# A Fourier layer with a routed feed-forward part: the first stage folded onto 64x64 tiles, its scratch tensor stored as twice 64 rows, and zero rows written from 120 partitions

## Chip, cores and metric

The kernel runs on one core of a Trainium2 chip. The metric is the time of one execution on the device in microseconds, given as the median of several runs. One execution was also profiled.

## The reference

```python
def _attn_ref(x, w_r, w_i, b_r, b_i):           # x: 8 x 3136 x 256
    X = np.fft.rfft(x, axis=1)
    Yr = Xr @ w_r - Xi @ w_i + b_r               # Xr, Xi: real and imaginary part
    Yi = Xr @ w_i + Xi @ w_r + b_i
    lam = 0.01                                   # soft threshold of both
    Yr = np.sign(Yr) * np.maximum(np.abs(Yr) - lam, 0.0)
    Yi = np.sign(Yi) * np.maximum(np.abs(Yi) - lam, 0.0)
    return np.fft.irfft(Yr + 1j * Yi, n=3136, axis=1)

def _moe_ref(x, w_gate, w1, w2, capacity):       # capacity 128, per batch
    scores = np.einsum('bsd,d->bs', x, w_gate)
    out = x.copy()
    top_idx = np.argpartition(-scores[b], capacity)[:capacity]
    h = np.maximum(x[b, top_idx] @ w1, 0.0)
    out[b, top_idx] = x[b, top_idx] + sigmoid(scores[b, top_idx])[:, None] * (h @ w2)
```

## The kernel before

A sequence of 3136 samples is taken as 98 rows of 32 (`N1`, `N2`), and the transform is done in two stages each way. For each of the 8 batches:

- **First stage**, `ld_x` and `s1`: an x tile holds 98 rows on partitions and 8 of the 32 columns, each of 256 channels. One batch has four tiles and eight units (`U`); a unit multiplies four columns by the 98x98 table `w` (line 400, two matmuls of 512 columns in float32) into the PSUM tile `s` and copies it out (line 405). After every second unit the result goes to the scratch tensor `As` in DRAM (lines 411 and 412: 96 rows and 2 rows).
- **Second stage** and the work in the frequency domain, per group g of 13 (`G`): `ld_a` loads `av` from `As` with the columns on partitions, one load for two groups; `s2` makes the spectrum (line 446, PSUM tile `px`), split into a high part `Xh` (ScalarE, 452) and a low part `Xl` (VectorE, 453); `spectral` multiplies by the weights (lines 228 to 230): a common product into `pcb`, copied by ScalarE to `ks` (467), from which GpSimd makes `kb` (469, with the bias), and two products into `py`, to which VectorE adds `kb` (473). `shrink` gives `Y` (ScalarE 478, VectorE 480). `s2i` transforms back into `pca` and `pcb` (498), ScalarE copies them to `ct` (505), VectorE forms the scores (`junk`, 507), and `ct` goes to the scratch tensor `Cs`.
- **Last stage**, `ld_c` and `s1i`: 128-row tiles `cv` of `Cs` (twice 64 rows, of which 49 count) are multiplied by `wi_sb` as four matmuls of 49 rows on quarters of the array (line 556), copied (558) and stored to the output.
- **Routing**: `select` and `place` find the 128 highest scores on VectorE with small matmuls, then GpSimd gathers the rows, two matrix products follow, and the rows are scattered back.

The order of each engine's work is the order of the code. The main loop runs over steps t, one group each: step t issues the stores left by step t - 1 (`flush`), loads, then `s2(t + 1)`, a unit of `s1` or `s1i` (`pair`), `spectral(t)`, the late DMAs on ScalarE's queue, `s2i(t - 1)`, `shrink(t)` and a second unit. Batches 2 to 7 of the first stage run `LEAD` = 17 steps ahead of their groups, about eight units in 13 steps, at t = 9 to 87; the units of batch 1 stand in steps 1 to 8, those of batch 0 ahead of the loop. The x loads stand four steps ahead of the unit, `av` is loaded at t + 3 and has two buffers, x has three.

Nearly all DMAs are issued by SP, in program order; `move` puts every other half of the output on ScalarE's queue instead. DMAs take eight semaphores in turn, so each waits until the eighth before it has landed. At t = 3 `pads` writes zeros into rows 49 to 63 of each half of the three `Cs` tensors, which the last stage loads with the rest: 15 rows of 32 KB six times, all from 15 partitions of one zeroed tile. `warm` runs matmuls and transposes at the very start, while the first x tiles are loaded.

Of the kernel before, what the change touches and what calls it, by code (L numbers as in the profile page):

```python
# [27 lines left out]
def _tables():  # L28
    m = np.arange(NH)
    n2 = np.arange(N2)  # L30
    n4 = np.arange(64)
# [4 lines left out]
    wi = np.zeros((64, 64))
    g = np.zeros((2, 2, N2, NJ - 1, 3, N2))
    gi = np.zeros((2, 2, N2, NP, 2, 2, 64))
    for j in range(NJ - 1):
        e = 2 * j + 2  # L40
        for p, r in enumerate((e, NH - e if e < NH else 0)):
            a = 2 * np.pi * ((n1 * r) % N1) / N1
            wf[:, j, p, 0] = np.cos(a)
            wf[:, j, p, 1] = -np.sin(a)
            for k2 in range(N2):
                k = r + 98 * k2
                sg = 1.0 if 2 * k <= S else -1.0
# [56 lines left out]
def fourier_moe(ctx: ExitStack, tc: tile.TileContext, x, w_r, w_i, b_r, b_i, wg, w1, w2,  # L104
# [21 lines left out]
    w = c_tile([N1, N1], F32, "w")  # L126
# [3 lines left out]
    xts = [c_tile([128, 8, D], F32, "xt" + str(k)) for k in range(3)]  # L130
    cvs = [c_tile([128, 8, D], F32, "cv" + str(k)) for k in range(2)]
# [251 lines left out]
    def ld_x(b, i):  # L383
        if i % 2:
            return
        k = i // 2
        t = xt[b, k] = (xts[:2] + cvs)[k] if b == 0 else xts[(4 * b + k + 1) % 3]
        ld(t[:96], xv[b, :96, 8 * k:8 * k + 8, :])
        ld(t[96:N1], xv[b, 96:, 8 * k:8 * k + 8, :])

    def s1(b, i):
        if i == 0:
            As[b] = dram.tile([N1, N2, D], F32, name="As")
        if i % 2 == 0:
            at[b] = pool.tile([128, 2, 2, 2 * D], F32, name="ot" if b == 0 and i > 3 else "at", bufs=2)
        f = xt[b, i // 2]
# [5 lines left out]
        if b == 0 and i % 2:  # L402
            nc.vector.tensor_copy(t[:N1, i % 2], p[:N1])
        else:
            nc.scalar.copy(out=t[:N1, i % 2], in_=p[:N1])  # L405
# [3 lines left out]
        def store():  # L409
            n = slice(4 * i - 4, 4 * i + 4)  # L410
            nc.sync.dma_start(out=As[b][:96, n, :], in_=t[:96])
            nc.sync.dma_start(out=As[b][96:, n, :], in_=t[96:N1])
        stores.append(store)

    def ld_a(b, g):
        if g == G - 1:
            av[b, g] = pool.tile([64, 1, D], F32, name="av", bufs=2)
            ld(av[b, g][:, 0, :], As[b][96:].rearrange("c n d -> (c n) d"))
        elif g % 2 == 0:
            av[b, g] = av[b, g + 1] = pool.tile([128, 4, D], F32, name="av", bufs=2)  # L420
            ld(av[b, g], As[b][:96].rearrange("(j c) n d -> (c n) j d", c=4)[:, 2 * g:2 * g + 4])

    def s2(b, g):
# [27 lines left out]
        vh, vl = [t.rearrange("p h c (j a s) -> p a (h c) j s", j=2, a=2) for t in (xh, xl)]  # L451
# [82 lines left out]
    def pads():  # L534
        z = pool.tile([128, 2, 2, 2 * D], F32, name="ot", bufs=2).rearrange("p r s (o x) -> p o (r s x)", o=1)
# [32 lines left out]
    def warm():  # L568
# [7 lines left out]
        a = pool.tile([128, 2, 2, 2 * D], F32, name="ot", bufs=2).rearrange("p a b c -> p (a b c)")  # L576
        nc.gpsimd.memset(a, 0.0)
        v = a.rearrange("p (n d) -> p d n", d=64)[:, :16]
        nc.vector.transpose(out=v, in_=v)
        nc.vector.transpose(out=a[:, :512], in_=a[:, :512])  # L580
        nc.vector.transpose(out=v, in_=p[:, 0].rearrange("p (n d) -> p d n", d=16))
        nc.vector.transpose(out=a[:, :512], in_=p[:, 1])

    YB, XB, KB, RB = 2, 2, 1, 1
# [94 lines left out]
    rest = [(b, i) for b in range(B) for i in range(U)]
    for t in range(-1, B * G + 20):  # L680
# [19 lines left out]
        if t == 3:  # L700
            pads()
# [66 lines left out]
```

## Time and profile before

| | |
|---|---|
| median of 3 runs | 826.88 us (819.29 to 827.66) |
| profiled execution | 832.16 us, span of its instructions 830.4 us |
| TensorE, matmuls | 711.4 us busy, 86% |
| VectorE | 478.4 us, 58% |
| ScalarE | 366.7 us, 44% |
| GpSimd | 161.1 us, 19% |
| DMA | 174.46 MB, mean 210 GB/s |
| granted TensorE clock, mean | 0.930 of full |

How to read it: the busy share is a mean over stages. Matmuls overlap, so their times are given as the union of the intervals. A wait counts only where the waiting engine is the one that the rest waits for; a row of the waits names the engine, the line and the releaser inferred from semaphores.

### The profile page before, as it was taken

What the parts mean: (1) busy time and instruction counts of PE and PEld (TensorE: products, weight loads), DVE (VectorE), ACT (ScalarE), POOL (GpSimd) and SP (SyncE); (2) the same over time, 40 slices, a digit from 0 to 9 for tenths busy, and PEclk for the clock granted to TensorE, in tenths of its full rate; (3) what the DMA queues carried; (4) which work ended last, traced back from release to release, by engine and by line L of the source; (5) the groups of instructions that cost most, each with busy time, mean ns of one, the idle gap of its engine ahead of it and who ended that gap; (6) DMA issues with size and microseconds to landing.
All of it is one profiled execution on the core that took longest, in us unless ns stands there. A gap on an engine that the chain in (4) does not pass through costs nothing. (4 is left out here: it accounts for less than half of the span.)

```text
span 830.4 us, 19603 instructions
## 1 busy us (share of the span) xinstructions
PE 711.4 (86%) x7964; PEld 516.1 (62%) x7964; DVE 478.4 (58%) x1333; ACT 366.7 (44%) x663; POOL 161.1 (19%) x148
## 2 busy tenths in 40 slices
PE   8189159999889998999899999999899789878876
PEld 4067137767666666666677677666677677654464
DVE  3335115555446776756646776766548989871640
ACT  2035115555545555545544554655454444432200
POOL 0013012212212221212212212222212122220000
PEclk9679659999999999999999999999999999895679
DMA  9749886679878978878778786888666455557600
GB/s 244 242 141 208 130 260 191 165 249 290 303 229 231 297 217 253 264 217 246 236 235 242 223 240 209 276 247 254 213 194 211 150 167 169 160 151 276 144 18 13
DMA packets 78266, 174.46 MB, mean 210 GB/s; under 512 B 6427, under 2 KB 59640, under 8 KB 67448
## 3 DMA queue, kind: packets, MB, share of 16 engines
q1 hardware_dynamic: 73440, 158.38, 64.1%
q10 hardware_dynamic: 3840, 12.66, 5.5%
q0 software_dynamic: 896, 2.17, 0.9%
q8 instruction: 63, 1.03, 0.5%
q14 instruction: 27, 0.22, 0.1%
HBM read 92.18 MB, written 81.07 MB: 209 GB/s over the span
## 5 line engine op out<-in xcount | busy, mean ns | idle before, releaser
L469 POOL TENSOR_TENSOR kb<-ks,bias 128x512 f32<-128x512 f32 (+1 forms) x104 | 134.1, 1289 | 572.7 <-ACT ks L467 572.7
L473 DVE TENSOR_TENSOR py<-py,kb 128x512 f32<-128x512 f32 (+1 forms) x104 | 72.4, 696 | 129.3 <-POOL kb L469 117.8
L446 PE MATMUL px<-g_sb,av 64*64 64x96 f32 x3072 | 85.9, 248 | 63.3 <-DMA av<-As 41.6
L453 DVE TENSOR_TENSOR Xl<-px,Xh 128x768 fp32r<-128x768 f32 x96 | 91.9, 957 | 72.6 <-ACT Xh L452 72.3
L446 PEld LDWEIGHTS px<-g_sb,av 64*64 64x64 f32 x3072 | 79.0, 136 | 85.4 <-issue 71.1
L505 ACT COPY ct<-pcb 128x256 f32<-128x256 f32 x96 | 35.7, 371 | 199.8 <-PE pcb L498 195.9
L400 PE MATMUL s<-xt,w 98*98 98x512 f32 x232 | 116.4, 625 | 4.3 <-ACT ot L558 4.3
L452 ACT CAST Xh<-px 128x768 fp32r<-128x768 f32 x96 | 77.3, 806 | 64.2 <-PE px L446 64.0
L498 PE MATMUL pca<-Y,gi_sb 64*64 64x256 f32 x768 | 104.4, 391 | 0.0
L498 PE MATMUL pcb<-Y,gi_sb 64*64 64x256 f32 x768 | 104.4, 391 | 0.0
L405 ACT COPY at<-s 98x1024 f32<-98x1024 f32 x58 | 58.9, 1015 | 48.3 <-PE s L400 34.0
L478 ACT ACTIVATE r<-py,m2l 128x512 f32<-128x512 f32 (+1 forms) x104 | 72.5, 697 | 11.5 <-DVE py L473 11.5
L228 PE MATMUL pcb<-wsh,Xh 128*128 128x256 f32 x208 | 76.1, 366 | 0.6 <-DVE Csc L507 0.6
L556 PE MATMUL s<-cv,wi_sb 49*64 49x512 f32 x464 | 68.6, 622 | 6.9 <-ACT ot L558 6.9
L480 DVE SCALAR_TENSOR_TENSOR Y<-py,r 128x512 f32<-128x512 f32 (+1 forms) x104 | 71.2, 685 | 2.1 <-ACT r L478 2.1
L558 ACT COPY ot<-s 128x1024 f32<-128x1024 f32 x58 | 59.2, 1021 | 15.8 <-PE s L556 15.6
L507 DVE CUSTOM_DVE_ANT_0 junk<-pcb,wgb 128x256 f32<-128x256 f32 x96 | 40.5, 422 | 40.9 <-ACT ct L505 40.0
L498 PEld LDWEIGHTS pca<-Y,gi_sb 64*64 64x64 f32 x768 | 45.8, 133 | 26.7 <-issue 2.4
L400 PEld LDWEIGHTS s<-xt,w 98*98 98x98 f32 x232 | 34.2, 166 | 43.6 <-issue 32.2
L228 PE MATMUL py<-wnh,Xh 128*128 128x256 f32 x208 | 59.7, 287 | 0.6 <-DVE Y L480 0.6
L230 PE MATMUL pcb<-wsl,Xh 128*128 128x256 f32 x208 | 59.7, 287 | 0.0
L229 PE MATMUL pcb<-wsh,Xl 128*128 128x256 f32 x208 | 59.7, 287 | 0.0
(135 smaller groups left out, 1369.8 us busy)
## 6 DMA issues: line engine op xcount, KB each, us to landing
cv<-Cs SPq DMA_DIRECT2D x30, 1024.0 KB
av<-As SPq DMA_DIRECT2D x48, 512.0 KB
Cs<-ct SPq DMA_DIRECT2D x96, 256.0 KB
xt<-in_x SPq DMA_DIRECT2D x30, 768.0 KB
As<-at SPq DMA_DIRECT2D x30, 768.0 KB
out<-ot SPq DMA_DIRECT2D x30, 384.0 KB
out<-ot ACTq DMA_DIRECT2D x30, 384.0 KB
Cs<-ot SPq DMA_DIRECT2D x6, 480.0 KB
```

The source lines that it names most:

```text
L228: nc.tensor.matmul(out, wh, mh, start=start, stop=False)
L229: nc.tensor.matmul(out, wl, mh, start=False, stop=False)
L400: nc.tensor.matmul(p[:N1, h, :], w, f[:N1, n:n + 2, :], start=True, stop=True)
L446: nc.tensor.matmul(o[:, :, N2 * j:N2 * j + N2], a[64 * p:64 * p + 64, 2 * (g % 2) + j, 128 * h + 64 * q:128 * h + 64 * q + 64], g_sb[64 * ...
L452: nc.scalar.copy(out=vh, in_=v)
L453: nc.vector.tensor_tensor(out=vl, in0=v, in1=vh.bitcast(F32), op=ALU.subtract)
L469: nc.gpsimd.tensor_tensor(out=kb[:r], in0=ks[:r].broadcast_to([r, 2, D]), in1=bias[:r], op=ALU.add)
L473: nc.vector.tensor_tensor(out=py[:r], in0=py[:r], in1=kb[:r], op=ALU.add)
L478: nc.scalar.activation(out=r1[:r], in_=py[:r], func=AF.Relu, bias=m2l[:r], scale=1.0)
L480: nc.vector.scalar_tensor_tensor(out=y[:r], in0=py[:r], scalar=0.0, in1=r1[:r], op0=ALU.min, op1=ALU.add)
L498: nc.tensor.matmul(p[q][64 * a:64 * a + 64], gi_sb[64 * q:64 * q + 64, g, c, 64 * a:64 * a + 64], y[64 * q:64 * q + 64, c, :], start=(c == ...
L556: nc.tensor.matmul(p[64 * c:64 * c + 64, r, :], wi_sb[64 * r:64 * r + NH], f[64 * r:64 * r + NH, 4 * c + 2 * e:4 * c + 2 * e + 2, :], star ...
```

## The change

- **Fold.** x rows m and m + 49 are added and subtracted (`fold`, two `tensor_tensor` per unit), and the 98-row product becomes two 49-row products, of the sums (c = 0, even rows of the spectrum) and the differences (c = 1, odd ones). A tile has 128 partitions in two halves r of 64, each with four of the tile's columns, so a unit is four matmuls of 49 rows by 64 results on quarters of the array, the form of line 556. Rows 49 to 63 of the tiles are zeroed once. In batch 0 two of three folds run on VectorE, all others on GpSimd, after `spectral` of the step two ahead of the unit.
- **As** has twice 64 rows and is stored with one DMA of 128 partitions; `av` is loaded with two DMAs for two groups (one for each half q), at t + 4 and with three buffers (`AB`).
- **x** is loaded as two halves of 48 rows, the second through `move` on ScalarE's queue, and one DMA for the rows 48; it has two buffers for three.
- **Zero rows** are written from 120 partitions (15 rows of 32 KB, cut into 120 pieces of 4 KB), a pair of DMAs in each of the steps 8, 10 and 12.
- The first stage's copies all run on ScalarE (in batch 0 every second one ran on VectorE); `warm` stands behind the first units and keeps only its matmuls. The tables are reordered to match.

```diff
-    xts = [c_tile([128, 8, D], F32, "xt" + str(k)) for k in range(3)]
-    cvs = [c_tile([128, 8, D], F32, "cv" + str(k)) for k in range(2)]
+    xts, cvs = [[c_tile([128, 8, D], F32, n + str(k)) for k in range(2)] for n in ("xt", "cv")]
+    for k, t in enumerate(xts + cvs):
+        (nc.vector if k % 2 else nc.gpsimd).memset(t[32:64], 0.0)
...
-        ld(t[:96], xv[b, :96, 8 * k:8 * k + 8, :])
-        ld(t[96:N1], xv[b, 96:, 8 * k:8 * k + 8, :])
+        for r in (1, 0):
+            move(r, t[64 * r:64 * r + 48], xv[b, :48, :, 8 * k + 4 * r:8 * k + 4 * r + 4, :])
+        ld(t[48:113:64], xv[b, 48, :, 8 * k:8 * k + 8, :].rearrange("h (r c) d -> r h c d", r=2))
+
+    def fold(b, i, eng):
+        e = i % 2
+        t = xt[b, i // 2][:, :, 2 * e:2 * e + 2, :]
+        f = sd[b, i] = pool.tile([128, 2, 2, D], F32, name="sd", bufs=2)
+        for k, op in enumerate((ALU.add, ALU.subtract)):
+            eng.tensor_tensor(out=f[:113, k], in0=t[:113, 0], in1=t[:113, 1], op=op)
...
-        for h in range(2):
-            n = 4 * (i % 2) + 2 * h
-            nc.tensor.matmul(p[:N1, h, :], w, f[:N1, n:n + 2, :], start=True, stop=True)
+        for r in range(2):
+            for c in range(2):
+                nc.tensor.matmul(p[64 * c:64 * c + 64, r, :], w[64 * r:64 * r + NH, c, :], f[64 * r:64 * r + NH, c], start=True, stop=True)
...
-            nc.sync.dma_start(out=As[b][:96, n, :], in_=t[:96])
-            nc.sync.dma_start(out=As[b][96:, n, :], in_=t[96:N1])
+            nc.sync.dma_start(out=As[b].rearrange("q m n d -> (q m) n d")[:, 4 * i - 4:4 * i + 4, :], in_=t)
...
-            av[b, g] = av[b, g + 1] = pool.tile([128, 4, D], F32, name="av", bufs=2)
-            ld(av[b, g], As[b][:96].rearrange("(j c) n d -> (c n) j d", c=4)[:, 2 * g:2 * g + 4])
+            av[b, g] = av[b, g + 1] = pool.tile([128, 2, 2, D], F32, name="av", bufs=AB)
+            for q in range(2):
+                ld(av[b, g][:, q], As[b][q, :48].rearrange("(j c) n d -> (c n) j d", c=4)[:, g:g + 2])
...
-        for t in Csd:
-            for q in range(2):
-                ld(t[q, NH:].rearrange("m n d -> m (n d)").rearrange("m (k x) -> m k x", k=4), z[:64 - NH].broadcast_to([64 - NH, 4, 2048]))
+        for q in range(2):
+            ld(Csd[k][q, NH:].rearrange("m n d -> (m n d)").rearrange("(p x) -> p x", p=120), z[:120, :1024])
...
-        if 1 < t + 3 < B * G:
-            ld_a(*divmod(t + 3, G))
+        if 1 < t + 4 < B * G:
+            ld_a(*divmod(t + 4, G))
...
-        if t == 3:
-            pads()
+        if t in (8, 10, 12):
+            pads((t - 8) // 2)
...
         issue_late()
+        for b, i in steady(t + LEAD + 2):
+            fold(b, i, nc.gpsimd)
```

What this moves on SP, steps 3 and 4 of the kernel before (`av<-As` is the second-stage load, `Cs<-ot` the zero rows, `at` the first stage's result):

```order
L155 DMA av<-As 128x4x256 [waits DMAHW5_49]
L155 DMA gi_sb<-t_gi 128x512 [waits DMAHW6_49]
L155 DMA Cs_70<-ot 60x1x2048 [waits DMAHW7_49,Pool_49]
L155 DMA Cs_71<-ot 60x1x2048 [waits DMAHW1_49]
L155 DMA Cs_72<-ot 60x1x2048 [waits DMAHW3_49]
L155 DMA g_sb<-t_g 128x384 [waits DMAHW5_49]
L411 DMA As<-at 96x2048 [waits DMAHW6_49,Activation_49]
L412 DMA As<-at 2x2048 [waits DMAHW7_49]
```

There each `Cs<-ot` row stands twice. Of the change, steps 7 and 8:

```order
L153 DMA gi_sb<-t_gi 128x512 [waits DMAHW6_49]
L159 DMA xt_78<-in_x 48x2x1024 [waits DMAHW7_49,Pool_49]
L153 DMA xt_78<-in_x 2x2x1024 [waits DMAHW0_49]
L153 DMA av<-As 32x256 [waits DMAHW2_49,PE_49]
L153 DMA gt_sb<-t_gt 64x192 [waits DMAHW4_49]
L153 DMA Cs_70<-ot 120x1024 [waits DMAHW5_49,Pool_49]
L153 DMA wq<-t_wq 25x392 [waits DMAHW7_49]
```

The zero rows now stand behind all second-stage loads of the first batch, one `Cs` tensor at a time.

GpSimd in the steady steps, before (`kb` of one group after the other, here around the last group of a batch):

```order
L469 TENSOR_TENSOR kb<-ks,bias 128x512 x3
L431 MEMSET Xh 128x6x64
L431 MEMSET Xl 128x6x64
L469 TENSOR_TENSOR kb<-ks,bias 128x512
L469 TENSOR_TENSOR kb<-ks,bias 64x512
```

and with the change, from the same place on (`sd` is the folded tile):

```order
L434 MEMSET Xl 128x6x64
L472 TENSOR_TENSOR kb<-ks,bias 128x512
L395 TENSOR_TENSOR sd<-xt_78 113x512 x2
L472 TENSOR_TENSOR kb<-ks,bias 64x512
L472 TENSOR_TENSOR kb<-ks,bias 128x512
L395 TENSOR_TENSOR sd<-xt_77 113x512 x2
L472 TENSOR_TENSOR kb<-ks,bias 128x512 x2
```

Between two `kb` there are now two adds in eight steps of 13.

ScalarE in a step that loads the last x tile of a batch (t = 40), with the change:

```order
L560 COPY ot<-s 128x2x512 [waits DMAHW5_49,DMAHW4_49,PE_49]
L470 COPY ks<-pcb 128x256 [waits PE_49,Pool_49]
L163 DMA out<-ot 96x1x1024 [waits DMAHW4_49,Activation_49]
L163 DMA xt_78<-in_x 48x2x1024 [waits DMAHW0_49]
L508 COPY ct<-pcb 128x256 [waits DMAHW1_49,PE_49]
L508 COPY ct<-pca 128x256 [waits DVE_49]
L481 ACTIVATE r_3575<-py,m2l 128x512 [waits DVE_49]
L455 CAST Xh<-px 128x2x6x64 [waits PE_49]
```

The `xt` row is new on this queue; before, only the `out` row stood there.

## Rows read from the trace of the kernel before

**Rows 1.** The page's first part: engine, busy us, share of the span, instructions.
```profile
PE 711.4 (86%) x7964; PEld 516.1 (62%) x7964; DVE 478.4 (58%) x1333; ACT 366.7 (44%) x663; POOL 161.1 (19%) x148
```

**Rows 2.** Stages: stretch, us, busy PE PEld DVE ACT POOL, clock, DMA share, GB/s.
```profile
44.00:112.00 68.00, 40.76 (x490) 30.47 (x484) 21.80 (x47) 22.00 (x40) 10.69 (x8) 0.78 0.75 168
112.00:138.00 26.00, 25.59 (x264) 18.55 (x264) 10.15 (x22) 11.80 (x21) 5.96 (x10) 0.84 0.65 194
138.00:620.00 482.00, 453.15 (x5491) 327.18 (x5490) 296.46 (x812) 256.56 (x465) 106.12 (x93) 0.99 0.79 241
620.00:720.00 100.00, 87.60 (x1200) 71.25 (x1198) 88.22 (x230) 46.02 (x92) 23.42 (x20) 0.98 0.57 175
720.00:831.00 111.00, 84.20 (x465) 58.80 (x465) 47.88 (x205) 24.31 (x40) 12.94 (x13) 0.77 0.41 121
```

**Rows 3.** TensorE's waits: releaser, us in total, times, longest us.
```profile
PE px L446 <- DMA av<-As: 41.6, 9, 25.8
```

**Rows 4.** TensorE's timeline: start, us, instruction, in brackets the idle time before.
```profile
43.23 1.56 PE L446 MATMUL px<-g_sb,av 64*64 64x96 f32 x32 [19.78 <-issue]
...
112.41 1.56 PE L446 MATMUL px<-g_sb,av 64*64 64x96 f32 x32 [25.75 <-DMA av<-As]
...
121.96 0.84 PE L446 MATMUL px<-g_sb,av 64*64 64x96 f32 x32
...
127.65 0.84 PE L446 MATMUL px<-g_sb,av 64*64 64x96 f32 x32
```

**Rows 5.** SP's timeline around the zero rows: start, us of issue, DMA, count.
```profile
67.52 0.50 SPq L155 DMA_DIRECT2D gi_sb<-t_gi  x1
68.12 19.53 SPq L155 DMA_DIRECT2D Cs<-ot  x6
87.70 4.89 SPq L155 DMA_DIRECT2D g_sb<-t_g  x1
...
103.69 0.96 SPq L155 DMA_DIRECT2D xt<-in_x  x2
104.69 0.39 SPq L155 DMA_DIRECT2D av<-As  x1
```

**Rows 6.** Short stretches, columns as in rows 2.
```profile
24.00:31.00 7.00, 0.00 (x0) 0.00 (x0) 5.52 (x11) 0.00 (x0) 0.00 (x0) 0.81 1.03 239
...
88.00:100.00 12.00, 0.00 (x0) 0.00 (x0) 0.74 (x3) 0.00 (x0) 0.00 (x0) 0.58 0.86 108
...
112.00:116.00 4.00, 3.59 (x35) 2.27 (x36) 0.96 (x1) 0.80 (x1) 0.00 (x0) 0.50 1.03 386
116.00:120.00 4.00, 4.00 (x15) 2.92 (x15) 0.00 (x0) 1.38 (x2) 0.56 (x1) 0.50 1.09 283
...
756.00:764.00 8.00, 8.00 (x36) 4.40 (x35) 0.96 (x7) 1.76 (x2) 0.00 (x0) 0.50 1.00 399
```

**Rows 7.** TensorE's timeline, a unit of each kind and what follows it.
```profile
415.87 1.07 PE L556 MATMUL s<-cv,wi_sb 49*64 49x512 f32 x8
416.87 0.29 PE L523 MATMUL pca<-ident,Csc 128*25 128x128 f32 x1
...
421.81 1.96 PE L400 MATMUL s<-xt,w 98*98 98x512 f32 x4
423.70 0.53 PE L530 MATMUL pca<-sct,wq 25*98 25x32 f32 x4
```

**Rows 8.** Timeline of VectorE, ScalarE's DMA queue and GpSimd around 403 us.
```profile
402.56 0.35 DVE L314 SCALAR_TENSOR_TENSOR hot<-iota,end,hot 98x128 f32<-98x128 f32 x1
...
402.70 0.58 ACTq L165 DMA_DIRECT2D out<-ot  x1
...
403.07 1.28 POOL L469 TENSOR_TENSOR kb<-ks,bias 128x512 f32<-128x512 f32 x1 [5.27 <-ACT ks L467]
...
403.15 1.35 DVE L314 SCALAR_TENSOR_TENSOR hot<-iota,end,hot 98x128 f32<-98x128 f32 x1
```

**Rows 9.** ScalarE's waits for an output store: us in total, times, longest us.
```profile
ACT ct L505 <- DMA out<-ot: 3.9, 1, 3.9
```

More of the change, by code (lines that the diff above doesn't have):

```diff
@@ L114, in fourier_moe @@
     dram = ctx.enter_context(tc.tile_pool(name="scratch", bufs=3, space=bass.MemoryType.DRAM))
-    xv = x.rearrange("b (a c) d -> b a c d", c=N2)
+    xv = x.rearrange("b (h m c) d -> b m h c d", h=2, c=N2)
     ov = [o.rearrange("(a r k c e i) d -> c a k r (e i d)", r=2, k=4, c=2, e=2, i=2) for o in outs]
-    As, Cs, xt, at, ct, av, cv, ot, X, Y, Csc = [{} for _ in range(11)]
+    As, Cs, xt, sd, at, ct, av, cv, ot, X, Y, Csc = [{} for _ in range(12)]
     pca, pcb = [ps.tile([128, 2 * D], F32, name=n, bufs=1) for n in ("pca", "pcb")]
@@ L386, in ld_x @@
         k = i // 2
-        t = xt[b, k] = (xts[:2] + cvs)[k] if b == 0 else xts[(4 * b + k + 1) % 3]
-        ld(t[:96], xv[b, :96, 8 * k:8 * k + 8, :])
-        ld(t[96:N1], xv[b, 96:, 8 * k:8 * k + 8, :])
+        t = xt[b, k] = (cvs if b == 0 and k > 1 else xts)[k % 2].rearrange("p (h c) d -> p h c d", h=2)
+        for r in (1, 0):
[7 more added lines that the diff above has]
+            eng.tensor_tensor(out=f[:113, k], in0=t[:113, 0], in1=t[:113, 1], op=op)
     def s1(b, i):
         if i == 0:
-            As[b] = dram.tile([N1, N2, D], F32, name="As")
+            As[b] = dram.tile([2, 64, N2, D], F32, name="As")
         if i % 2 == 0:
             at[b] = pool.tile([128, 2, 2, 2 * D], F32, name="ot" if b == 0 and i > 3 else "at", bufs=2)
-        f = xt[b, i // 2]
+        f = sd.pop((b, i))
         p = ps.tile([128, 2, 2 * D], F32, name="px" if b == 0 and i % 2 else "s", bufs=1)
-        for h in range(2):
-            n = 4 * (i % 2) + 2 * h
-            nc.tensor.matmul(p[:N1, h, :], w, f[:N1, n:n + 2, :], start=True, stop=True)
+        for r in range(2):
+            for c in range(2):
+                nc.tensor.matmul(p[64 * c:64 * c + 64, r, :], w[64 * r:64 * r + NH, c, :], f[64 * r:64 * r + NH, c], start=True, stop=True)
         t = at[b]
[L402 to L405, printed above, removed]
+        nc.scalar.copy(out=t[:, :, i % 2, :], in_=p)
         if i % 2 == 0:
@@ L450, in s2 @@
         v = px[:, :, :384].rearrange("p a (k j s) -> p a k j s", k=6, j=2)
[L451 removed]
+        vh, vl = [t.rearrange("p h c (a j s) -> p a (h c) j s", j=2, a=2) for t in (xh, xl)]
         nc.scalar.copy(out=vh, in_=v)
@@ L532, in score, with pads @@
         nc.vector.tensor_copy(scores[:, b, :], p)
-    def pads():
-        z = pool.tile([128, 2, 2, 2 * D], F32, name="ot", bufs=2).rearrange("p r s (o x) -> p o (r s x)", o=1)
+    def pads(k):
+        z = pool.tile([128, 2, 2, 2 * D], F32, name="ot", bufs=2).rearrange("p r s x -> p (r s x)")
         nc.gpsimd.memset(z, 0.0)
-        for t in Csd:
-            for q in range(2):
-                ld(t[q, NH:].rearrange("m n d -> m (n d)").rearrange("m (k x) -> m k x", k=4), z[:64 - NH].broadcast_to([64 - NH, 4, 2048]))
+        for q in range(2):
+            ld(Csd[k][q, NH:].rearrange("m n d -> (m n d)").rearrange("(p x) -> p x", p=120), z[:120, :1024])
     def ld_c(b, i):
@@ L575, in warm @@
             nc.tensor.matmul(p[:, i % 2], pr[:, :128], pr[:, :512], start=True, stop=True)
[L576 to L584, printed above, removed]
+    YB, XB, KB, RB, AB = 2, 2, 1, 1, 3
     G, U = 13, 8
@@ L661, in steady @@
         return due(u, U) if u >= 2 * G else []
-    warm()
     for i in range(U):
         ld_x(0, i)
+    issue_late()
     consts_a()
@@ L668, in fourier_moe @@
     for i in range(U):
+        fold(0, i, nc.gpsimd if i % 3 == 2 else nc.vector)
         s1(0, i)
@@ L672, in fourier_moe @@
             ld_x(1, 2)
-            ld_x(1, 4)
         flush()
+        issue_late()
     weights()
+    warm()
     ld_a(0, 0)
+    ld_a(0, 2)
     consts_g(1)
     first = {i + 1: i for i in range(U)}
+    fold(1, 0, nc.gpsimd)
+    fold(1, 1, nc.gpsimd)
     rest = [(b, i) for b in range(B) for i in range(U)]
@@ L683, in fourier_moe @@
             ld_x(b, i)
-        if t + 4 in first and first[t + 4] > 5:
+        if t + 4 in first and first[t + 4] > 3:
             ld_x(1, first[t + 4])
-        if 1 < t + 3 < B * G:
-            ld_a(*divmod(t + 3, G))
+        if 1 < t + 4 < B * G:
+            ld_a(*divmod(t + 4, G))
         for b, i in due(t - LAG + 2, U):
@@ L727, in fourier_moe @@
         issue_late()
+        for b, i in steady(t + LEAD + 2):
+            fold(b, i, nc.gpsimd)
+        if t + 2 in first and first[t + 2] > 1:
+            fold(1, first[t + 2], nc.gpsimd)
         tick(ffns)
```

38 lines of the change are left out of this document (17 added, 21 removed).

## The prediction

> **What bounds the kernel now.** I read the engines first, then the stages, then the waits. TensorE is busy for 711.4 us of a span of 830.4, VectorE 478.4, GpSimd 161.1 [rows 1], so the first question is where TensorE is not busy. The stages say it [rows 2]: between 138 and 620 us it works 453 of 482 us at full clock, so there each microsecond of TensorE's work counts nearly whole; between 44 and 112 us it works only 40.8 of 68; from 620 on no first-stage unit is left, and from 720 on the routing of the last batch and its output take 111 us that the edit does not touch.
>
> The hole in the second stage is one wait: 25.8 us before the matmuls that read `av`, out of 41.6 us in nine such waits [rows 3]. TensorE resumes at 112.41 us [rows 4], on a load that SP issued at 104.69. SP had not got to it earlier because from 68.12 us it stood in the six zero-row DMAs of `pads`, 19.53 us of issue alone, and in what queued behind them until 104 [rows 5]. While nothing else ran, 88 to 100 us, the DMA engines were 0.86 busy and moved 108 GB/s; filling `av` later, in 756 to 764 us, 128-partition loads of `cv` and `xt` ran at 399 [rows 6]. So it is a slow transfer, and SP's order hands its slowness to TensorE. After the hole TensorE runs at a granted 0.50 for some 8 us [rows 6].
>
> **The change part by part**, against the profiled execution's own 832.16 us (span 830.4); the median of the three runs, 826.88, lies 5.28 below it.
>
> *Zero rows.* Six DMAs of 480 KB from 15 partitions become six of 480 KB from 120, in three pairs at steps 8, 10 and 12 instead of all at step 3. 2.95 MB at 108 GB/s are 27 us, which is the hole. At the rate of the wide loads in [rows 6] (399) a pair takes 2.5 us, at 108 it would still take 9; the pairs are two steps apart, and 120 partitions are nearest to 128, so I take 3. With it goes the hole, 25.75 us, and the slow restart: the step that begins at 112.41 lasts 9.55 us, the next one 5.69 [rows 4], 3.86 more. What comes back: with the hole closed, the first 13 steps take about 13 x 4.9 = 64 us and must move, by the shapes in the code, 5 x loads (4.0 MB), 5 As stores of 1.05 MB (5.2), av (3.2), Cs (2.6), the g and gi tables (2.7), the pads (2.95) and some 0.2 MB: 20.9 MB. In the steady stage 241 GB/s go with a DMA share of 0.79 [rows 2], so 305 GB/s would be full: 68.5 us. That is 4.5 us too much, and bursts cost more: I take 8 (0, if it runs at the 399 of wide transfers, to 20, at 250 GB/s). Term: -25.8 - 3.9 + 8 = **-21.6** (-29.6 to -9.6).
>
> *First stage as 64x64 tiles.* Two full matmuls of 98 rows become four of 49 rows on four quarters of the array, which is the very form of the inverse stage (`s1i`), so its price stands in the trace: a first-stage unit fills 421.81 to 423.70, 1.89 us; an inverse unit 415.87 to 416.87, 1.00 us [rows 7]. Where a unit runs straight into the next product the difference is nearer 0.75, so I take 0.8. The eight units of batch 0 stand in the DMA-bound start and give nothing; the other 56 give 8 x 0.8 = 6.4 in the second batch's first steps and 48 x 0.8 = 38.4 in the steady stage. Term: **-44.8**, if nothing else takes TensorE's place.
>
> *`av` one step earlier, three buffers.* Without the big hole, 41.6 - 25.8 = 15.8 us of waits for `av` remain in eight places [rows 3], about 2 us each. Loading a step (some 5 us) earlier should end most: **-12** (0 to -15.8).
>
> *The folds on GpSimd.* Two adds per unit, on 113 x 512 elements; the nearest row is `kb`, 128 x 512, 1.28 us, so 2.56 per unit. GpSimd stands 5.27 us idle before the next `kb` [rows 8]; a fold fits even when the step is 0.8 shorter, with some 2 us over. Cost 0, and if that cover is gone (a fold that waits for x), what is late next is `kb`, then the VectorE add that waits for it, then `Y`, then the products.
> Against it stands a lock that the trace shows: `hot<-iota,end,hot`, 0.35 us alone, took 1.35 when `kb` began 0.08 us before it [rows 8]. With three times the adds on GpSimd such meetings become more frequent; each costs VectorE at most 1.0 us, and VectorE is idle 186 of 482 us in that stage [rows 2]. I take 3 (0 to 12). The Trainium skill has the rule behind it (SBUF — State Buffer, section "Who interferes with whom"): a VectorE instruction with two SBUF inputs and a GpSimd instruction that reads SBUF hold the shared port in turn, one blocks for the whole of the other, while one with a single SBUF input is free. The trace agrees for the two-input form. By the rule the long VectorE instructions (`Xl`, `py`, `Y`, one input from PSUM) stay free; no row here shows them beside a GpSimd add, which is the third rival.
>
> *x in halves, one of them issued on ScalarE.* A DMA instruction holds ScalarE's queue 0.58 us [rows 8]; 24 of them lie in the steady stage, where ScalarE is idle for nearly half the time [rows 2]. But in this program DMAs take eight semaphores in turn, and each waits for the eighth before it; for one tile in each batch the eighth is the As store of the same step, and ScalarE, in order, waits for it to land. Behind it stand the copies of `pcb` and `pca`, `r` and `Xh`, that is `Y` and the next step. Such a wait is seen once before, 3.9 us [rows 9]. I take 5 for six batches (0 to 6 x 3.9 = 23). The rate of the halves is not in the trace: x tiles now go at 239 GB/s, 24 to 31 us [rows 6], and I take the same for the halves (108 to 399 as bounds).
> The Trainium skill speaks against this one (SBUF — State Buffer, section "Can I just issue two DMAs to hit both halves?"): two DMAs on the two partition halves gain about 6% over one. With its 196 GB/s for 64 partitions a 0.80 MB tile would take an estimated 4.1 us for the 3.4 of the row; no run here shows it yet, and it matters only if DMA becomes the limit.
>
> *As of 128 rows.* 0.98 MB more per batch, 5% more traffic in a stage that shrinks by a tenth: the share goes from 0.79 to about 0.92. Late loads are the price; I take 5 (0 to 25). SP's queue hardly grows (423 rows to 447: two av loads for one, one As store for two).
>
> *Start.* TensorE waits 19.78 us until 43.23 [rows 4] for the last As stores, behind transfers that fill the queues. One x tile fewer is ahead of them (-3.4 us at 239 GB/s), four stores of 0.25 MB more (+2.5 at 399), two memsets and a fold stand in the chain (+3). Term **+2** (-4 to +6). The warm-up is moved, and the clock will have fallen again before the first real product.
>
> Sum: -21.6 - 44.8 - 12 + 3 + 5 + 5 + 2 = -63.4, so 768.8 on the profiled scale and **763.5** as a median of runs.
>
> **Rivals.**
> 1. *The transfers give half of it back.* As rows and halves make loads late in bursts; the steady stage gives 25 of its 37, the first steps lose 20 and half of 6.4: 832.2 - 9.6 - 3.2 - 25 + 2 = 796, as a median **791**. For it: the share of 0.92. Against: full is still 482 x 0.79 x 1.05 = 400 us of transfers for some 440 us.
> 2. *All covers hold*: -29.6 - 44.8 - 15.8 - 2 = 740 on the profile, **735** as a median. For it: the 399 GB/s of wide transfers. Against: the first 13 steps then move 330 GB/s without a pause.
> 3. *Slower: a fold blocks VectorE's PSUM instructions too.* The fold starts where `kb` ends, which is where `py`, the `junk` sums, `Y` and `Xl` begin. If each of them must wait for a GpSimd add, a fold adds 2.56 us to its step: 56 x 2.56 = 143 us against 63 gained: **about 906**. It decides from 1.1 us per fold on (63 / 56). Against it: the rule above.
> 4. *A fold waits for its x tile and holds `kb`.* Loads lead the fold by two steps, some 10 us, where the matmuls used to follow by four; SP and ScalarE issue them in order. With about 2 us over, a tile that is 4.5 us late each time eats 24 x 2.5 = 60 us: **about 824**, no change. Against: `cv` has the same two steps now and its units wait for nothing but ScalarE.
>
> **How the numbers follow.** The sum 0.61, with its own range 748 to 780; rival 1 0.18, rival 2 0.12, rival 3 0.04, rival 4 0.05. A measurement of this kernel tells about 1% from no change (8 us). Faster by over 1%: 0.61 + 0.18 + 0.12 = 0.91; within 1%: 0.05; slower: 0.04. The range for 8 in 10 goes from rival 2's upper part to rival 1: 738 to 795.
>
> **What would show it.** Zero rows: no wait of over 5 us for `av` after the first step, and the full clock from the first steps to 620 us or its new end. Tiles: units of `s` at 1.0 us from start to the next product. Cover: `kb` starting right after `ks`, POOL busy about 325 us; `Xl` still 0.96 and `Y` 0.69 us. ScalarE: waits for DMA of under 10 us in all. I would be wrong if POOL waits for x tiles, if ScalarE waits for lanes in each batch, or if the steady stage keeps its length while TensorE's busy time falls.

## The result and the profile after

The changed kernel takes **800.56 us** (median of four runs, 798.99 to 802.64) beside 825.88 us (819.29 to 827.66) for the kernel before: a ratio of 0.9709, interval 0.965 to 0.9768. The forecast was 763.5 us, with a range of 738 to 795. The direction was right; the gain is 25 us where 63 were forecast, and the time lies 5.6 us above the range. Here and below medians are of all runs of a kernel, while ratios and their intervals leave out those that lay over 1.5% above its fastest.

The first part of the page of the changed kernel (engine, busy us, share of the span, instructions) answers to [rows 1]:

```profile
PE 675.1 (85%) x8220; PEld 502.5 (63%) x8220; DVE 522.9 (65%) x1339; ACT 365.3 (46%) x667; POOL 309.7 (39%) x267
```

TensorE works 36.3 us less where 44.8 were forecast, and GpSimd's 309.7 is near the forecast 325. VectorE, which the edit gives no work in the steps, is 44.5 us longer busy.

The stages of the changed kernel, with columns as in [rows 2] and bounds at about the same points of the program, the second and third row there taken together:

```profile
48.00:112.00 64.00, 59.47 (x837) 45.80 (x837) 34.19 (x76) 34.50 (x66) 41.55 (x38) 0.91 0.94 278
112.00:590.00 478.00, 422.87 (x5578) 318.66 (x5579) 331.35 (x798) 248.04 (x456) 218.07 (x183) 0.95 0.85 257
590.00:690.00 100.00, 88.24 (x1217) 71.08 (x1215) 88.64 (x231) 47.80 (x94) 22.61 (x20) 1.00 0.58 172
690.00:799.00 109.00, 82.16 (x516) 58.24 (x514) 50.56 (x212) 24.96 (x42) 13.77 (x14) 0.80 0.43 128
```

The hole ahead of the second-stage matmuls, which fell in the first of these stretches, is gone: TensorE is busy 59.5 of 64 us there. The long stage is where the forecast failed. Its length is best read from the last group's matmuls, which read `gt_sb` once in each batch; "first and last start" bounds batches 0 to 7. The row before, the row after, then the same stretch as a window (columns as in [rows 2]), before and after:

```profile
L434 PE MATMUL px<-gt_sb,av x64: 322/322/323, 139.0 to 728.8; 64*64 64x192 f32 x64
```
```profile
L437 PE MATMUL px<-gt_sb,av x64: 322/323/337, 109.6 to 701.8; 64*64 64x192 f32 x64
```
```profile
139.00:728.80 589.80, 546.88 (x6722) 404.02 (x6720) 390.37 (x1061) 304.56 (x560) 131.87 (x116) 0.99 0.75 228
```
```profile
109.60:701.80 592.20, 522.14 (x6906) 398.63 (x6904) 430.72 (x1061) 300.28 (x560) 247.22 (x209) 0.95 0.80 241
```

Up to the first of these points the kernel gained 29.4 us (139.0 to 109.6). Over the seven batches behind it, here called the **steady stage**, it gained nothing: 592.2 us for 589.8. Behind the last point it gained 4.5 (101.6 to 97.1). That makes the 31.5 us by which the two profiled spans differ; the medians differ by 25.3, as the profiled execution of the kernel before took 832.16 us, 6.3 above its median. TensorE's idle time there (length less busy time) rose from 42.9 to 70.1 us, and the granted clock fell from 0.99 to 0.95.

What TensorE waits for in that stretch (us in total, times, longest us), changed kernel:

```profile
PE pca L254 <- DVE Csc L510: 26.3, 18, 2.7
PE s L558 <- ACT ot L560: 19.0, 9, 3.5
PE pca L317 <- DVE Csc L510: 7.4, 4, 3.4
PE s L406 <- ACT ot L560: 5.7, 5, 1.5
PE s L558 <- DMA cv<-Cs: 5.0, 3, 2.2
```

`av`, which took 15.9 us of this stage before, is not among them. The waits are for VectorE and for ScalarE's `ot` copy, and ScalarE itself is late through VectorE (its waits in the same stretch):

```profile
ACT r L481 <- DVE py L476: 35.6, 26, 3.0
```

One step shows the chain. VectorE's, GpSimd's and TensorE's timelines from 302 us (start, us, instruction, idle time before in brackets), and three short windows of that step:

```profile
302.24 1.27 DVE L269 SCALAR_TENSOR_TENSOR w<-d,w 98x2 uint32<-98x2 uint32 x1
303.55 1.20 DVE L243 TENSOR_TENSOR f<-digits,w 98x6 uint32<-98x6 uint32 x1
304.79 1.38 DVE L247 TENSOR_TENSOR c<-scores,f 98x192 bf16<-98x192 f32 x1
306.20 0.35 DVE L251 TENSOR_REDUCE n<-c 98x6 bf16<-98x192 bf16 x1
306.47 0.69 DVE L476 TENSOR_TENSOR py<-py,kb 128x512 f32<-128x512 f32 x1
```
```profile
302.22 1.28 POOL L472 TENSOR_TENSOR kb<-ks,bias 128x512 f32<-128x512 f32 x1 [1.42 <-ACT ks L470]
303.45 2.50 POOL L395 TENSOR_TENSOR sd<-xt 113x512 f32<-113x512 f32 x2
```
```profile
304.38 1.04 PE L406 MATMUL s<-sd,w 49*64 49x512 f32 x8
308.12 0.17 PE L254 MATMUL pca<-n,tm 98*98 98x6 bf16 x1 [2.70 <-DVE Csc L510]
```
```profile
302.00:305.50 3.50, 3.42 (x64) 2.27 (x63) 3.36 (x5) 0.79 (x3) 3.28 (x3) 1.00 0.99 291
305.50:308.10 2.60, 0.00 (x0) 0.00 (x0) 2.42 (x8) 0.85 (x2) 0.45 (x1) 1.00 0.97 362
308.10:312.90 4.80, 4.78 (x39) 4.16 (x42) 4.50 (x9) 1.71 (x3) 1.28 (x1) 0.64 0.70 250
```

In a step where GpSimd does not stand beside them, the same three of VectorE's instructions are short (timeline from 296.3 us):

```profile
296.38 0.16 DVE L269 SCALAR_TENSOR_TENSOR w<-d,w 98x2 uint32<-98x2 uint32 x1
296.57 0.17 DVE L243 TENSOR_TENSOR f<-digits,w 98x6 uint32<-98x6 uint32 x1
...
296.78 0.36 DVE L247 TENSOR_TENSOR c<-scores,f 98x192 bf16<-98x192 f32 x1
```

From 302.24 us on each lasts about as long as one GpSimd add: `w` beside `kb`, `f` beside the first half of the fold, `c` beside the second. Together 3.85 us for 0.69. Behind them in VectorE's queue stand `n`, which the select's matmul needs, `py`, which ScalarE's `r` needs, and `junk`, which frees `pca`. TensorE runs dry at 305.4, sits 2.70 us, and comes back at a granted 0.64 over 4.80 us, a mix of its two levels of 1.2 and 2.4 GHz. So such a step costs twice: as idle time and as slow matmuls behind it.

### The profile page after: what moved, and what is told of

It reads as the page before. It is cut to its first block, busy times and chain, and to the rows that moved or that the text cites. A ratio compares the mean times of both kernels' runs of the same rounds, so it can differ in the third digit from the quotient of the medians.

```text
span 798.9 us, 20430 instructions
## 1 busy us (share of the span) xinstructions
PE 675.1 (85%) x8220; PEld 502.5 (63%) x8220; DVE 522.9 (65%) x1339; ACT 365.3 (46%) x667; POOL 309.7 (39%) x267
## 5 line engine op out<-in xcount | busy, mean ns | idle before, releaser
L395 POOL TENSOR_TENSOR sd<-xt 113x512 f32<-113x512 f32 x114 | 143.3, 1278 | 25.8 <-DMA xt<-in_x 25.8
L406 PE MATMUL s<-sd,w 49*64 49x512 f32 x480 | 69.6, 623 | 19.9 <-DVE sd L395 14.2
L226 PE MATMUL pcb<-wsh,Xh 128*128 128x256 f32 x208 | 70.8, 341 | 2.0 <-DVE Csc L510 2.0
L226 PEld LDWEIGHTS pcb<-wsh,Xh 128*128 128x128 f32 x208 | 41.4, 199 | 46.2 <-issue 25.5
L408 ACT COPY at<-s 128x1024 f32<-128x1024 f32 x58 | 60.3, 1039 | 17.2 <-PE s L406 17.2
L226 PE MATMUL py<-wnh,Xh 128*128 128x256 f32 x208 | 63.4, 305 | 1.0 <-DVE Y L483 0.9
L227 PE MATMUL py<-wnh,Xl 128*128 128x256 f32 x208 | 62.2, 299 | 0.0
```

Of the source, the lines that this page charges most:

```text
L226: nc.tensor.matmul(out, wh, mh, start=start, stop=False)
L395: eng.tensor_tensor(out=f[:113, k], in0=t[:113, 0], in1=t[:113, 1], op=op)
L406: nc.tensor.matmul(p[64 * c:64 * c + 64, r, :], w[64 * r:64 * r + NH, c, :], f[64 * r:64 * r + NH, c], start=True, stop=True)
```

## The experiments

**Theory A:** GpSimd's adds hold VectorE's routing, `py` comes late, TensorE waits and then runs slowly. **Theory B:** the extra transfers (share 0.80 for 0.75) and the waits for DMA lanes eat the gain. In the windows below the stretch is each kernel's own steady stage, columns as in [rows 2].

**1. The zero rows alone**

```diff
 # kernel before
-        if t == 3:
-            pads()
+        if t in (8, 10, 12):
+            pads((t - 8) // 2)        # the changed kernel's pads(k), 120 partitions
```

> The kernel before with the new zero rows alone (three pairs of DMAs from 120 partitions at steps 8, 10 and 12). The forecast's own term for them was -21.6 us, bounds -29.6 to -9.6. Theory A (the steady stage of the changed kernel, 592.2 us from the last group of batch 0 to the last group of batch 7 against 589.6 before, has lost its whole gain to VectorE instructions that wait for GpSimd's adds) says that nearly all of the measured -25 us is this edit: 826 - 25 = 801 us, steady stage 585 to 592 us. Theory B (the changed kernel's transfers take the gain back) says the same of this run; it tells apart what the zero rows are worth alone from the forecast's bounds. If the start term was the loser instead, this run is below 797.

```profile
109.30:698.10 588.80, 546.04 (x6724) 402.85 (x6722) 391.45 (x1061) 304.73 (x561) 133.71 (x117) 0.99 0.75 232
```

Measured: 794.18 us beside 827.26, ratio 0.9573 (0.9509 to 0.9637). The profiled execution took 801.5 us, the upper end of its four, so its stages are read and not its total. The start is as short as the changed kernel's (109.3), the steady stage is that of before. This one edit gives 33 us by the medians and 35 by the ratio, more than the whole change. All the rest of the change together cost 6 to 10 us by the medians (800.56 and, measured again, 804.20) and 11 to 14 by the ratios. The edit changes both the width of the transfers and their place; which of the two did it was not tried apart. For the width speaks that SyncE issues a pair of them in 0.79 us, where it stood 19.53 us in the six before [rows 5].

**2. No folds in the steps**

```diff
 # changed kernel, units of batches 1 to 7; the fold calls in the loop are gone
-        f = sd.pop((b, i))
+        f = xt[b, i // 2][:, :, 2 * e:2 * e + 2, :]
```

> The changed kernel without the folds of batches 1 to 7: the units read the rows of x as loaded, so the sums and differences of the two halves of x are left out; every DMA, matmul and copy stays. Theory A (lock): VectorE's w, f, c, hot go back to about 0.40, 0.27, 0.49, 0.25 us, TensorE's idle time in the steady stage halves, the clock goes back to 0.98 or more, steady stage 552 to 560 us, total 762 to 768 us. Theory B (transfers near their limit, waits for DMA lanes on SyncE and ScalarE): nothing changes but GpSimd's busy time, 798 to 803 us.

```profile
138.60:695.50 556.90, 509.68 (x6908) 388.28 (x6905) 403.11 (x1061) 300.00 (x560) 133.35 (x117) 0.98 0.85 255
```

Measured: 797.65 us, ratio 0.9657 (0.9608 to 0.9706). By the total theory B would win, but the steady stage is 556.9 us, just as theory A said; what undid it is the start, 138.6 for 109.6, where without folds TensorE's units wait for their tiles (20.3 us for `xt` loads between 50 and 151 us). The experiment changed two things, and run 5 repeats it without the second.

**3. Late folds**

```diff
 # changed kernel, in the loop, behind py's add
+        if todo and 0 <= t < B * G:
+            nc.gpsimd.memset(kb[:1, 0, :1], 0.0)   # waits until VectorE's py add has read kb
         for b, i in todo:
             fold(b, i, nc.gpsimd)
```

> The changed kernel with the folds held on GpSimd until VectorE's py add of the same step is done (a one-element GpSimd write to kb, which that add reads, stands ahead of the folds). The same adds, the same DMAs; only their place in the step changes: they lie beside junk, Y and Xl, which have one input in PSUM. Theory A: w, f and c meet only kb, as before the change; steady stage 555 to 565 us, total 765 to 775 us. Theory B: 798 to 803 us. If the added wait holds kb of the next step: over 805 us.

> The changed kernel once more, beside the next three on one chip: 797 to 804 us.

> The kernel with late folds once more, beside the others on one chip: 766 to 780 us, that is 20 to 34 us below the changed kernel.

```profile
109.50:677.20 567.70, 512.09 (x6907) 388.57 (x6904) 401.23 (x1061) 300.44 (x560) 253.14 (x255) 0.98 0.84 252
```

Measured: 775.36 us, ratio 0.9308 (0.9227 to 0.9389); once more beside the changed kernel on one chip, 770.59 for 804.20 (ratios 0.9373 and 0.9738). The same adds and the same transfers, moved to another place in the step, give 25 and 34 us. That fits A and not B. Whether the folds hold VectorE by reading SBUF or only by keeping GpSimd busy is left to run 5.

**4. No x loads from batch 2 on**

```diff
 # changed kernel, ld_x
+        if b > 1:
+            return
```

> The changed kernel without the loads of x from batch 2 on: the folds and units of batches 2 to 7 use what lies in the tiles, so six of eight batches of x are left out. 48 MB x 0.4 = 19.3 MB of 182 MB less, and no x DMA on ScalarE's queue in the steady stage. Theory A: the folds still meet VectorE's instructions, w, f, c keep 0.75, 0.54, 0.85 us, total 792 to 801 us. Theory B: the share of DMA falls by a tenth, the waits for lanes go, steady stage 555 to 565 us, total 763 to 775 us.

```profile
107.50:693.70 586.20, 521.68 (x6908) 397.67 (x6906) 430.62 (x1061) 300.33 (x561) 247.32 (x209) 0.95 0.68 214
```

Measured: 796.62 us, ratio 0.9642 (0.9582 to 0.9701). The DMA share falls from 0.80 to 0.68, and the steady stage gives 6 us. TensorE's idle time is still 64.5 us, and the clock 0.95. Theory B is not the main cause.

**5. GpSimd as busy, without reading SBUF**

```diff
 # changed kernel, fold, batches 2 to 7
-        for k, op in enumerate((ALU.add, ALU.subtract)):
-            eng.tensor_tensor(out=f[:113, k], in0=t[:113, 0], in1=t[:113, 1], op=op)
+        for k in range(3):
+            eng.memset(f[:113], 0.5)
```

> The changed kernel with each fold of batches 2 to 7 (two adds, 2.56 us of GpSimd) replaced by three writes of a constant into the same tile (by the 1.81 us of a 128x2048 write, 2.7 us in all), so the sums of x are left out there; GpSimd is as busy in the same places, waits and DMAs of the units stay, but nothing is read from SBUF. The start is that of the changed kernel, which the run without folds did not keep. Theory A (VectorE waits while GpSimd reads SBUF): w, f, c back to 0.40, 0.27, 0.49 us, steady stage 552 to 560 us, total 761 to 769 us. Rival (GpSimd's occupancy itself: kb late, or its place in the queue): steady stage 585 to 595, total 795 to 803 us.

Its window, then the groups of VectorE's instructions `c`, `w` and `f` (count, busy us, mean ns, idle before) of the kernel before, of the changed kernel and of this one:

```profile
110.00:667.90 557.90, 507.35 (x6908) 385.74 (x6906) 406.14 (x1061) 300.47 (x561) 261.85 (x255) 0.98 0.84 256
```
```profile
L249 DVE TENSOR_TENSOR c<-scores,f 98x192 bf16<-98x192 f32 (+4 forms) x70 | 32.7, 468 | 1.9
L271 DVE SCALAR_TENSOR_TENSOR w<-d,w 98x2 uint32<-98x2 uint32 (+1 forms) x65 | 23.3, 358 | 2.2
L245 DVE TENSOR_TENSOR f<-digits,w 98x6 uint32<-98x6 uint32 (+3 forms) x65 | 15.9, 245 | 2.3
```
```profile
L247 DVE TENSOR_TENSOR c<-scores,f 98x192 bf16<-98x192 f32 (+4 forms) x70 | 45.3, 647 | 1.9
L269 DVE SCALAR_TENSOR_TENSOR w<-d,w 98x2 uint32<-98x2 uint32 (+1 forms) x65 | 38.7, 595 | 2.3
L243 DVE TENSOR_TENSOR f<-digits,w 98x6 uint32<-98x6 uint32 (+3 forms) x65 | 23.3, 358 | 2.2
```
```profile
L269 DVE SCALAR_TENSOR_TENSOR w<-d,w 98x2 uint32<-98x2 uint32 (+1 forms) x65 | 41.0, 631 | 2.2
L247 DVE TENSOR_TENSOR c<-scores,f 98x192 bf16<-98x192 f32 (+4 forms) x70 | 31.0, 442 | 1.9
L243 DVE TENSOR_TENSOR f<-digits,w 98x6 uint32<-98x6 uint32 (+3 forms) x65 | 13.0, 200 | 2.2
```

Measured: 772.51 us (763.09 to 775.96), ratio 0.937 (0.9286 to 0.9454); the median is 3.5 us above the expected window, the steady stage, 557.9, inside it. The profiled execution was the fastest of its five, 9.4 us below the median, so the stage's gain is an upper end: by the medians the run gives 28 us. GpSimd is busier (261.9 for 247.2 us), and most of the loss is gone: 34.3 us of this execution's steady stage, of which TensorE's idle time gives 19.5 (70.1 to 50.6) and its busy time, the same work at a better clock, 14.8. So for `f` and `c`, which are short again, reading SBUF matters and not GpSimd's time. `w` is not short, as it still meets `kb`; what the meetings with `kb` cost is taken up in runs 11 and 12. The folds behind `kb` had made three meetings in a row.

**6. Both halves of x on SyncE**

```diff
 # kernel of run 3, ld_x
-            move(r, t[64 * r:64 * r + 48], ...)
+            ld(t[64 * r:64 * r + 48], ...)
```

> The kernel with late folds (775.4 us), with both halves of each x tile issued by SyncE instead of one of them by ScalarE. The forecast had +5 us (0 to 23) for ScalarE's half: if that term is right, 765 to 772 us. If ScalarE's half costs nothing or SyncE is the longer queue, 775 to 790 us; the steady stage, 566 us, says it apart from the start.

```profile
107.70:679.90 572.20, 513.75 (x6906) 389.38 (x6904) 399.16 (x1060) 300.96 (x560) 251.99 (x253) 0.97 0.84 250
```

Measured: 784.18 us, ratio 0.9497 (0.9414 to 0.9581), 9 to 14 us more than run 3, on another chip; the interval overlaps that of run 3's second measurement (0.9287 to 0.946), not that of the first. ScalarE's half is at least no loss against this arrangement, and by the medians a gain. Why is not shown: TensorE's waits for `cv` in the steady stage, 15.5 us, are about run 3's 14.4 below.

**7 and 8. Inverse units a step later, with late folds and alone**

```diff
-    LEAD, LAG = 17, 18
+    LEAD, LAG = 17, 19
-        for b, i in due(t - LAG + 2, U):       # ld_c
+        for b, i in due(t - LAG + 3, U):
```

> The kernel with late folds (775.4 us), with the inverse units one step later and their cv loads where they were, so each load has three steps instead of two. TensorE waits 14.4 us there for cv in seven places of the steady stage. If late transfers are what is left of the loss: steady stage 566 -> 553 to 558 us, last batch's output up to 4 us later, total 763 to 771 us. If those waits only cover others (ScalarE's copies of ot, VectorE's routing): 773 to 780 us.

> The changed kernel with the inverse units one step later alone (folds as in the change). If late transfers and VectorE's waits for GpSimd are two separate losses, this gives what the later units gave on top of late folds, 8 to 13 us: 788 to 793 us. If the waits for cv lay under VectorE's lateness, nothing: 797 to 804. If VectorE's lateness was only what late cv units did to it: 770 to 780.

What TensorE waited for in run 3's steady stage, then run 7's window:

```profile
PE s L558 <- DMA cv<-Cs: 14.4, 7, 4.1
```
```profile
111.00:663.10 552.10, 503.19 (x6904) 382.98 (x6900) 398.18 (x1060) 300.46 (x560) 252.04 (x253) 0.99 0.83 257
```

Measured: with late folds **764.44 us** (763.69 to 765.55), ratio 0.9255 (0.9174 to 0.9336), the fastest version that computes the whole, 36 us below the changed kernel; alone 793.24, ratio 0.9612 (0.9529 to 0.9694), 11 us below the changed kernel beside it. So the place of the inverse units holds a second, smaller loss that adds to the first; behind late folds it was worth 6 to 11. Late `cv` loads are only part of it: in the changed kernel TensorE waits 5.0 us for them, and 19.0 for ScalarE's `ot` ahead of the same units. With the units a step later neither wait is left there, while the first-stage units' wait for `ot` goes from 5.7 to 14.7.

**9. av three steps ahead, two buffers**

```diff
 # kernel of run 3
-        if 1 < t + 4 < B * G:
-            ld_a(*divmod(t + 4, G))
+        if 3 < t + 3 < B * G:
+            ld_a(*divmod(t + 3, G))            # and AB = 2
```

> The kernel with late folds (775.4 us), with av loaded three steps ahead into two buffers, as before the change. The forecast's term for the earlier load was -12 us (0 to -15.8); the kernel before with the new zero rows waits 15.2 us for av in eight places of its steady stage. If that term is right: total 783 to 791 us, steady stage 576 to 582. If the earlier load only moves the waits to other transfers: 773 to 779 us.

Measured: 784.84 us, ratio 0.9503 (0.9418 to 0.9588). All of this kernel's waits for `av`, 6.3 us in run 3 (start alone), are

```profile
PE px L449 <- DMA av<-As: 23.7, 7, 8.0
```

The earlier load is worth 9 to 14 us, as forecast.

**10. Whole-array matmuls in the first stage**

```diff
 # kernel of run 7, s1, batches 1 to 7
-        for r in range(2):
-            for c in range(2):
-                nc.tensor.matmul(p[64 * c:64 * c + 64, r, :], w[64 * r:64 * r + NH, c, :], f[64 * r:64 * r + NH, c], ...)
+        for h in range(2):
+            nc.tensor.matmul(p[:, h, :], w[:113].rearrange("p c n -> p (c n)"), f[:113, h], ...)
```

> The kernel with late folds and later inverse units (764.4 us), with the matmuls of the units of batches 1 to 7 as two of 113 rows on the whole array instead of four of 49 rows on its quarters; the sums that they form are not those of the reference, their length is that of the kernel before. The forecast's price of the quarters was 0.8 us a unit, 44.8 us for 56. If it holds once VectorE is in time: 800 to 812 us, unit of s 1.9 us. If TensorE's time is hidden behind VectorE and transfers even then: 765 to 785 us.

```profile
115.50:691.10 575.60, 542.64 (x6722) 408.39 (x6716) 396.33 (x1061) 301.99 (x560) 252.69 (x255) 0.99 0.81 247
```

Measured: 788.70 us, ratio 0.9564 (0.9485 to 0.9643), 24.3 us above run 7, between the two expected windows. TensorE's busy time differs by 39.5 us, as the forecast's 48 x 0.8 = 38.4 said. But its idle time is 33.0 here and 48.9 with the quarters: 15.9 of the 39.5 us turn into waiting. The two runs are from different chips; the stages give 23.5 us (575.6 for 552.1), as the medians do.

**11 and 12. The same pair with kb written, not added**

```diff
 # kernels of run 7 and of run 10
-        nc.gpsimd.tensor_tensor(out=kb[:r], in0=ks[:r].broadcast_to([r, 2, D]), in1=bias[:r], op=ALU.add)
+        nc.gpsimd.memset(ks[:1, 0, :1], 0.0)
+        for k in range(2):
+            nc.gpsimd.memset(kb[:r], 0.01)
```

> The kernel with late folds and later inverse units (764.4 us), with kb made of two writes of a constant, as long as the add and started like it by ScalarE's ks, so the sum of ks and bias is left out; GpSimd then reads nothing from SBUF beside VectorE's routing. If the routing's waits for GpSimd are what still keeps TensorE idle (48.9 us of the steady stage): steady stage 552 -> 537 to 543 us, total 750 to 756. If VectorE's own chain and ScalarE's copies keep it: 760 to 766 us.

> The same with the first-stage matmuls as two on the whole array (788.7 us with the adds), so that the price of the quarters is taken without any SBUF read on GpSimd in the steps. If GpSimd's kb hides the other half of the quarters' 38 us: this run 786 to 790, 34 to 39 us above the run beside it. If VectorE's own chain and ScalarE's copies hide it: 20 to 26 us above the run beside it.

```profile
110.90:647.50 536.60, 504.09 (x6906) 383.04 (x6900) 366.54 (x1061) 298.44 (x560) 233.30 (x435) 0.99 0.85 265
```
```profile
117.50:677.30 559.80, 537.59 (x6720) 404.55 (x6716) 366.98 (x1061) 300.08 (x560) 233.10 (x435) 1.00 0.82 254
```

Measured: 747.64 us (ratio 0.9047, 0.8979 to 0.9115) and 774.34 (ratio 0.9359, 0.9293 to 0.9425). With `kb` written (1.14 us in all, for the add's 1.28) the kernels are 17 and 14 us faster, so `kb`'s own reads of SBUF cost up to that much; [rows 8] show such a meeting in the kernel before. In part it can be that `kb` ends 0.14 us sooner, which is 12.7 us over the 91 groups of the stage if all of it counted, as `py` waits for it; this was not tried apart. But the pair differs by 26.7 us, about as the other pair did: the quarters' other half does not hide behind that lock. The idle time still grows by 10.3 us with the quarters (22.2 to 32.5). What TensorE still waits for in run 11 is ScalarE's `ot` (12.5 us) and VectorE's `Csc` in the select (8.2), which points to their own chains in steps with routing; which link hides the quarters was not tried.

## Why the prediction was right or wrong

- **Zero rows:** right in that the hole goes, too small in size. -33 us for -21.6, outside its bounds (-29.6); the start alone gives 29.7 (139.0 to 109.3 in run 1). The 8 us for crowded first steps did not come: the changed kernel's first steps moved 278 GB/s at a share of 0.94 and TensorE was busy 59.5 of 64 us.
- **Quarters:** a unit fills 1.05 us where 1.0 was forecast, and between runs 7 and 10 TensorE's busy time differs by what was forecast (39.5 for 38.4); in the changed kernel's steady stage it fell by 24.7 only, as its clock fell too. The step that failed is "so there each microsecond of TensorE's work counts nearly whole", read from 453 busy of 482 us. Worth 24 us on the kernel of run 7 (27 without `kb`'s reads), not 44.8. The rows for the unit, from TensorE's timeline of the changed kernel:

```profile
293.58 1.04 PE L406 MATMUL s<-sd,w 49*64 49x512 f32 x8
294.63 0.17 PE L254 MATMUL pca<-n,tm 98*98 98x6 bf16 x1
```

- **`av` earlier:** right, -9 to -14 for -12.
- **The folds:** this step failed most. It was priced at +3 (0 to 12) from "each costs VectorE at most 1.0 us, and VectorE is idle 186 of 482 us in that stage". A single meeting did cost about that (1.11, 1.03 and 1.02 us above). But the fold is issued right behind `kb`, so three adds in a row meet three dependent instructions in a row; these stand ahead of `py` in VectorE's queue, so VectorE's idle time elsewhere did not cover them; and the sum had no term for the clock, which was 0.64 behind the gap above and fell from 0.99 to 0.95 over the stage. Measured by moving the folds: 25 to 34 us. The rival on this (VectorE's instructions with an input in PSUM blocked too, 906 us) was rightly set low: `Xl` keeps 0.96 us and `Y` 0.69. On this the Trainium skill (SBUF — State Buffer, section "Who interferes with whom") and the trace agree. But the prediction's "one with a single SBUF input is free" is too wide: that section of the Trainium skill frees it only outside VectorE's 2-port modes, which it says `copy` and `tensor_scalar` can enter, and the last section here shows one of each held. In which mode they ran no run shows.
- **x on ScalarE:** forecast +5; ScalarE's waits for a DMA sum to 10.7 us in the steps, in four places, but both halves on SyncE are 9 to 14 us slower. What SyncE's queue would take for that half was not priced; where the 9 to 14 us arise is open.
- **Late transfers:** +5 (0 to 25) forecast, 11 by run 8, which is not the transfers' alone: TensorE waited 5.0 us for `cv`, and what else that run moved are waits for `ot`. No first-stage unit waited for its x tile in the steps.
- **Start:** the first product begins at 48.30 instead of 43.23, +5.1 for +2. In the row below (changed kernel, TensorE) it waits for `av`:

```profile
48.30 1.03 PE L449 MATMUL px<-g_sb,av 64*64 64x96 f32 x17 [7.51 <-DMA av<-As]
```

With the measured terms the sum is -33 - 24 - 12 + 29 + 11 + 5 = -24, and 25 were measured; they were taken on different bases (other kernels, other chips, mid-points of ranges), so that they add up is in part luck: this is a tally and not a proof. The rival "transfers give half of it back" (791 us) came nearest in time, but by another mechanism: it let the transfers take 12 of the steady stage's 37 us and 20 in the first steps. At most 11 of the first can be theirs (run 8), the second did not come, and the folds' 25 to 34 us are not in it. The rival "A fold waits for its x tile and holds `kb`" did not occur: GpSimd waited for x tiles twice, both in the start. The text's own sign of error, "if the steady stage keeps its length while TensorE's busy time falls", is what happened.

## What to carry to other kernels

A cover must be looked for in the step and in the queue, not in a stage's mean: ask what stands behind the delayed instruction, and whether the new work is issued right behind the work that already delays it. Work moved to an engine that is free can still be placed within the step; here one wait that shifts it within the step was worth as much as the matmul saving. And price each part of a change alone where one can: one small edit, the zero rows, gave more than all of them together.

## What the runs showed of the hardware

- Not only instructions with two SBUF tensors are held by GpSimd's adds. The changed kernel's `mask` (min, median, max ns of one) reads a tile and a column of SBUF, and `thr` copies one tile; both show two lengths about a GpSimd add apart. At 333.56 us `thr` takes 1.29 us beside `kb` (333.54, 1.29), and the two `mask` behind it 1.21 and 1.30 beside the fold (334.79, 2.49). `Xl`, `junk<-pca` and `junk<-pcb`, which read PSUM beside one SBUF tile, keep their 957 and 423 ns in every instance of full size (at most 959 and 426), beside a fold too (`junk<-pca` at 300.01, the fold 298.29 to 300.81):

```profile
L278 DVE TENSOR_SCALAR mask<-scores,thr x8: 231/237/1209, 334.9 to 766.4; 98x32 bf16<-98x32 f32 x8
L279 DVE TENSOR_SCALAR mask<-scores,thr x8: 232/234/1310, 336.0 to 766.6; 98x32 bf16<-98x32 f32 x8
L272 DVE COPY thr<-w x5: 153/1282/1292, 333.6 to 766.2; 98x2 f32<-98x2 f32 x3, 98x1 f32<-98x1 f32 x2
```

- GpSimd's writes of a constant leave the instructions with two SBUF tensors free: `f` at 200 ns and `c` at 442 in run 5. In run 11, where `kb` is written and the folds still add, but late, `w` is at 161 ns, and VectorE's busy time in the steady stage falls from 398.2 (run 7) to 366.5 us. The writes do hold `thr` and `mask`. In run 5's step at 317 us `thr` lasts through the add of `kb` (317.12, 1.29) and the first of the three writes behind it, and a `mask` at 319.36 takes 0.98 us beside them; in run 11 `thr` takes 0.54 us beside a write of 0.52:

```profile
317.14 2.18 DVE L272 COPY thr<-w 98x2 f32<-98x2 f32 x1
```
```profile
318.35 2.96 POOL L396 MEMSET sd<- 113x1024 f32 x3
```

- After 2.60 us without a matmul the granted clock over the next 4.80 us was 0.64.
